# Another common order for 2210 operations of a gated recurrence with an MLP, on one core

## The chip, the cores and the metric

The kernel runs on one core of a Trainium2 chip. A core has five engines that run side by side, each with its own stream of instructions: TensorE (PE) for matrix products, VectorE (DVE) and ScalarE (ACT) for element-wise work, GpSimd (POOL) and SyncE (SP), which here mostly issue DMAs. An engine works through its stream strictly in the order in which the instructions were written down; where an instruction needs something of another engine, it waits for a semaphore, and all that stands behind it on its engine waits too. The metric is the device time of one execution in microseconds (us). A difference of 0.2% is about 1.1 us here.

## The reference

For 4 batches, 8 heads, 768 tokens and 48 channels a head, a gated linear recurrence with complex gates runs over the tokens; its output, laid side by side by heads (384 columns), goes through a low-rank mixing over the tokens (rank 32) and an MLP with a hidden width of 1536.

```python
mag = np.sqrt(a_re * a_re + a_im * a_im)
scale = np.minimum(mag, 0.999) / (mag + 1e-06)
a_re_n, a_im_n = (a_re * scale, a_im * scale)
for t in range(S):
    new_re = ar * S_re - ai * S_im
    new_im = ar * S_im + ai * S_re
    S_re, S_im = (new_re + kv, new_im)
    y[:, :, t] = np.einsum('bhd,bhde->bhe', q[:, :, t], S_re)
# x: y as (batch, token, head*channel)
h = xt @ U @ V
u = x + h.transpose(0, 2, 1)
ch = np.maximum(u @ w_ch1, 0.0) @ w_ch2
return u + ch
```

All of it is in 4-byte floats. `w_ch1` and `w_ch2`, `U` and `V` arrive as 8-byte floats and are turned into 4-byte ones on the chip.

## The kernel before

The 768 tokens of a batch are cut into chunks of 128; there are 24 chunks in all, six to a batch. Two neighbouring chunks make a group (`GROUPS`) for the gates, and two chunks make a token block for the MLP (`mixer`).

The work has these stages. `gates` (line 622) turns the gates of a group into logarithms of magnitudes and angles, sums both over the tokens of a chunk by a product with a triangle of ones (tiles `es ps` and `ph`), and takes exponentials and sines (tiles `es` and `cs`). `prep` (793) weighs the rows of q and k by `es` and `cs` (tiles `qk`, then `QKC`) and transposes them on PE, 16 small transposes at a time (tile `tr`, line 816), which ACT copies to `QK`. `chain` (827) has the products inside a half chunk (`inner`), the state that a chunk adds (`dk`), and the output (`y`), and ACT copies the output to `xo`. `mixer` (918) has the rank products (`rank`, `mixed`), the transposes of the token block (`uTp`), the first MLP layer (`up` for the first two token blocks, `few` for the others: a scheme with fewer products and more additions on DVE), and the second layer (`down`). The 8-byte weights come in by large loads into two staging areas (`single`, 555) and are converted by five instructions a piece, on DVE for the first six pieces and on DVE and ACT for the others. `judge` (1361) counts, from values collected by DVE all along (line 657), whether the inputs left the range for which the fast method holds: PE sums the counts (`count`), and DVE casts the sum to an integer in the tile `flag`. After all operations each engine loads `flag` into a register (line 1395) and branches on it (line 1405); the general method behind the branch does not run for these inputs.

None of these functions emits anything at once. Each call of `PE`, `ACT`, `DVE`, `POOL` or `SP` only registers an operation with the class `Plan`, with the names of what it reads and writes; from the names `Plan.add` works out which earlier operations it needs. Operations are numbered as they are registered, 0 to 2209. At the end the loop over `plan.order()` emits them in the sequence of the tuple `ORDER`, so this tuple fixes the stream of every engine: its operations in the sequence in which they stand in `ORDER`. `order()` also asserts that no operation stands before one that it needs, and that a buffer is not taken before its last user is listed. The waits between engines are not made from the names in the plan: they come from the tiles that the emitted instructions touch, so they are there whatever the plan says. The dictionary `SPARE` has PE emit 34 products without use ahead of operations 125, 135, 199, 209, 223 and 243 (`idle`, 1379), in both kernels.

The operations named below, by number: 91 to 94 load the gates of chunks 0 and 1, 0 loads the triangle, 5 and 11 the first two pieces of `w_ch1`, 18 and 17 `U` and `V`, 28 the third piece, 149 to 152 the gates of group 1, 194 and 195 q and k of chunk 0, 218 and 219 q and k of chunk 1, 196 v of chunk 0. 96 (ACT) and 97, 98 (DVE, lines 654 and 655) start the gates of chunk 0; 99 and 100 (DVE, line 657) collect its range check; 101 to 103 (ACT) and 104, 105 (DVE) end in the logarithm that 109 (PE, `es ps`) sums. 106 to 108 make the angles. 112 to 124 are the same for chunk 1, where 115 and 116 are the range check. 10 and 16 are the last conversions of the first two pieces of `w_ch1`. 198, 202, 222 and 226 (DVE, line 441) make `QKC` for q and k of chunks 0 and 1; 199, 203, 223 and 227 (PE) transpose them. 208 and 209 (`dk`) and 206 (`inner`) are the products of chunk 0. 368 makes `QKC` for k of chunk 4, 369 transposes it. 937, 1475 and 1968 are the rank products of batches 1 to 3. 2208 is the count on PE, 2209 the cast to `flag` on DVE.

Of the kernel before, what the change touches and what calls it, by code (L numbers as in the profile page):

```python
# [316 lines left out]
def kernel(  # L317
# [19 lines left out]
    DM = H * D  # L337
# [53 lines left out]
    def get(*base):  # L391
        if base not in T:
            T[base] = makers[base]()
        return T[base]
# [432 lines left out]
    def chain(i):  # L827
# [84 lines left out]
        for r in range(2):  # L912
            ACT(c_act(HH * D) + 0.04, RR, lambda r=r: nc.scalar.copy(out=halves(get(*xi))[r * HC:(r + 1) * HC, :, 1],
                                                                     in_=get(*y[1])[side(r, 1)]), [y[1] + (r,)], [xi + (r + 1,)])
# [540 lines left out]
```

## Time and profile before

| | us |
|---|---|
| device time, median of 3 runs | 554.59 |
| the runs | 554.28, 554.59, 554.6 |
| span of the profiled execution, first to last instruction | 552.8 |
| of it PE busy | 526.9 (95%) |
| PEld (weight loads, beside PE) busy | 477.3 (86%) |
| DVE busy | 432.8 (78%) |
| ACT busy | 317.8 (57%) |
| POOL busy | 32.2 (6%) |

For the profiled execution the profile gives the span alone, 552.8 us; the median of the runs, 554.59 us, lies 1.8 us above it, since a device time takes in what lies before the first and after the last instruction. The granted TensorE clock was 0.998 of full speed over the span.

In rows of the timeline the first number is the start in us from the beginning of the span, the second the length of the piece in us; then come the engine, the line of the kernel, the operation, the tiles (written <- read), the shape and the count, and in brackets the idle time of the engine before it and what ended it. Instructions of one engine overlap a little, so that the next one starts before the one before it has ended. Matrix products of 4-byte floats show as two records each.

### The profile page before, as it was taken

What the parts mean: (1) busy time and instruction counts of PE and PEld (TensorE: products, weight loads), DVE (VectorE), ACT (ScalarE), POOL (GpSimd) and SP (SyncE); (2) the same over time, 40 slices, a digit from 0 to 9 for tenths busy, and PEclk for the clock granted to TensorE, in tenths of its full rate; (3) what the DMA queues carried; (4) which work ended last, traced back from release to release, by engine and by line L of the source; (5) the groups of instructions that cost most, each with busy time, mean ns of one, the idle gap of its engine ahead of it and who ended that gap; (6) DMA issues with size and microseconds to landing.
All of it is one profiled execution on the core that took longest, in us unless ns stands there. A gap on an engine that the chain in (4) does not pass through costs nothing.

```text
span 552.8 us, 16672 instructions
## 1 busy us (share of the span) xinstructions
PE 526.9 (95%) x7228; PEld 477.3 (86%) x7228; DVE 432.8 (78%) x828; ACT 317.8 (57%) x553; POOL 32.2 (6%) x61
## 2 busy tenths in 40 slices
PE   2899999999999999999999999999999999999996
PEld 1677776767999987999999998999999989999995
DVE  6899989999999987998787987786953635567352
ACT  6889999795597787567827956626512232110100
POOL 1000000001010000102001001002000000000000
PEclk9999999999999999999999999999999999999999
DMA  9988876523441354314513425003300000000001
GB/s 229 187 184 174 195 170 151 144 30 87 88 89 30 56 104 77 59 31 85 91 38 67 74 38 111 2 1 59 59 9 23 17 11 15 8 8 23 21 9 34
DMA packets 150688, 39.92 MB, mean 72 GB/s; under 512 B 145912, under 2 KB 147408, under 8 KB 150608
## 3 DMA queue, kind: packets, MB, share of 16 engines
q1 hardware_dynamic: 148400, 34.43, 31.2%
q0 software_dynamic: 2208, 4.35, 2.3%
q8 instruction: 59, 0.97, 0.7%
q14 instruction: 21, 0.17, 0.1%
HBM read 33.60 MB, written 4.76 MB: 69 GB/s over the span
## 4 chain that ended last, share of the span: by engine, by line
PE 73%; DVE 12%; ACT 4%; issue 2%; DMA 1%; POOL 0%; DVEq 0%; SPq 0%; ACTq 0%; POOLq 0%
PE down L1235 26%; PE few L1103 25%; PE tr L816 4%; PE dk L865 3%; PE inner L845 3%; PE y L902 3%; PE up L991 2%; PE y L894 2%; DVE xo L444 1%; ACT gate L438 1%; PE rank L937 1%; PE ph L755 1%; PE mixed L960 1%; PE uTp L976 1%; PE es ps L691 1%
## 5 line engine op out<-in xcount | busy, mean ns | idle before, releaser
L1111 ACT COPY h<-few 128x512 f32<-128x512 f32 x60 | 35.1, 585 | 87.3 <-PE few L1103 87.1
L1235 PE MATMUL down<-w,h 128*128 128x192 f32 x396 | 72.7, 330 | 0.9 <-DVE xo L444 0.7
L438 ACT ACTIVATE gate<-gate 128x768 f32<-128x768 f32 (+2 forms) x74 | 65.6, 900 | 9.2 <-DVE GS L750 3.8
L1235 PEld LDWEIGHTS down<-w,h 128*128 128x128 f32 x396 | 64.5, 190 | 3.7 <-issue 1.5
L822 ACT COPY QK<-tr 112x512 f32<-112x512 f32 x96 | 49.9, 596 | 17.8 <-PE tr L816 17.7
L444 DVE TENSOR_TENSOR xo<-down,xo 128x192 f32<-128x192 f32 (+1 forms) x79 | 29.9, 385 | 33.9 <-PE down L1235 33.4
L1115 DVE CUSTOM_DVE_ANT_1 h<-few,h 128x512 f32<-128x512 f32 x60 | 40.5, 686 | 15.7 <-PE few L1103 11.8
L1103 PE MATMUL few<-extra,w 128*128 128x128 f32 x400 | 50.9, 276 | 0.0
L1103 PEld LDWEIGHTS few<-extra,w 128*128 128x128 f32 x400 | 48.0, 192 | 0.1
L441 DVE TENSOR_TENSOR QKC<-qk,cs 128x768 f32<-128x768 f32 x48 | 44.4, 950 | 1.7 <-PE dk L865 1.3
L1235 PE MATMUL down<-stage 128*128 128x192 f32 x198 | 37.9, 330 | 0.4 <-DVE xo L444 0.4
L438 ACT ACTIVATE es<-es ps 128x384 f32<-128x384 f32 x48 | 20.1, 502 | 31.2 <-PE es ps L691 29.2
L444 DVE TENSOR_TENSOR h<-few,h 128x512 f32<-128x512 f32 x30 | 20.6, 688 | 20.4 <-ACT h L1111 12.1
L1179 POOL DMA_DIRECT2D out_dram<-xo x32 | 17.9, 558 | 313.8 <-DVE xo L444 297.7
L991 PE MATMUL up<-uT,w 128*128 128x256 f32 x144 | 34.5, 387 | 0.7 <-ACT uT L980 0.7
L1235 PEld LDWEIGHTS down<-stage 128*128 128x128 f32 x198 | 32.3, 190 | 1.7 <-DVE xo L444 1.0
L1103 PE MATMUL few<-gate,w 128*128 128x128 f32 x240 | 32.2, 278 | 0.4 <-DVE gate L1075 0.4
L435 ACT ACT_TABLE_LOAD x24 | 30.8, 1283 | 1.1 <-PEq L1439 0.7
L816 PEld LDWEIGHTS tr<-ident,QKC 64*112 64x112 f32 x768 | 24.2, 130 | 8.3 <-issue 3.6
L816 PE MATMUL tr<-ident,QKC 64*112 64x64 f32 x768 | 28.9, 221 | 2.4 <-DVE QKC L441 2.4
L991 PEld LDWEIGHTS up<-uT,w 128*128 128x128 f32 x144 | 26.4, 190 | 5.3 <-ACT uT L980 0.9
L1103 PEld LDWEIGHTS few<-gate,w 128*128 128x128 f32 x240 | 29.3, 192 | 0.8 <-PE uTp L976 0.6
(161 smaller groups left out, 1100.4 us busy)
## 6 DMA issues: line engine op xcount, KB each, us to landing
stage<-in_moe_w_ch_dram SPq DMA_DIRECT2D x12, 768.0 KB
gate<-in_a_im_dram SPq DMA_DIRECT2D x24, 192.0 KB
gate<-in_a_re_dram SPq DMA_DIRECT2D x24, 192.0 KB
VP<-in_v_dram SPq DMA_DIRECT2D x24, 192.0 KB
qk<-in_q_dram SPq DMA_DIRECT2D x24, 192.0 KB
qk<-in_k_dram SPq DMA_DIRECT2D x24, 192.0 KB
out_dram<-xo POOLq DMA_DIRECT2D x12, 192.0 KB, 2.2
out_dram<-xo POOLq DMA_DIRECT2D x20, 96.0 KB, 2.1
```

Of the source, the lines that this page charges most:

```text
L435: ACT(1.4, rank, lambda: nc.scalar.preload_act_table_set(name), writes=[TABLE])
L438: return nc.scalar.activation(out=o, in_=i, func=f, **kw)
L441: nc.vector.tensor_tensor(out=o, in0=a, in1=b, op=OP.mult)
L444: nc.vector.tensor_tensor(out=o, in0=a, in1=b, op=OP.add)
L816: nc.tensor.transpose(out=get(*ps[r])[0:DQ, h], in_=get(*qkc)[at, h].rearrange("p u d -> p (u d)")[:, 0:DQ], identity=ident[at, at], tile_ ...
L822: nc.scalar.copy(out=get(*QK)[:, u].rearrange("p (h t) -> p h t", t=CH)[:, :, r * HC:(r + 1) * HC], in_=get(*ps[r])[0:DQ])
L991: nc.tensor.matmul(out=get(*ps)[:, e], lhsT=w1[:, f, (ff + e) * 128:(ff + e + 1) * 128], rhs=get(*uT)[:, f], start=(f == 0), stop=(f == KD ...
L1103: nc.tensor.matmul(out=get(*ps)[:, q], lhsT=w()[:, q * 128:(q + 1) * 128], rhs=v[0](), start=(n == 0 and q == 0), stop=True, skip_group_ch ...
L1111: ACT(c_act(n3 * CH) - 0.045, RU, lambda i=i, k=k: nc.scalar.copy(out=at(i, k), in_=get(*ps)), [ps], [o])
L1115: DVE(c_dve(n3 * CH), RU, lambda i=i, k=k: nc.vector._custom_dve(dve_ops.TENSOR_ADD_SAT, out=at(i, k), in0=get(*ps), in1=at(i, k), s0=math ...
L1179: queue.dma_start(out=out[b, c * CH:(c + 1) * CH, lo:hi], in_=get("xo", i)[:, lo:hi])
L1235: nc.tensor.matmul(out=get(*to)[:, part], lhsT=x(j), rhs=y[:, j], start=(first and j == 0), stop=(j == KH - 1), skip_group_check=not first)
```

## The change

The tuple `ORDER` is replaced by another permutation of the same 2210 numbers. Four registrations of operations get further names. The product that reads the piece of `w2` which one DVE instruction rewrites in place now reads a name, `("w2i", 0)`, that this instruction writes; the addition of a `down` product to `xo` reads the name of the PSUM bank as a whole; and the two copies from `y` read both halves of it. No operation is added or removed, none has another body, and each stays on its engine. The new tuple has one line more, so that line numbers below it rise by one.

```diff
 ORDER = (
-    95, 93, 91, 0, 92, 94, 196, 150, 5, 96, 99, 11, 3, 100, 4, 151, 97, 152, 101, 98, 149, 112, 115, 194, 116, 106, 218, 113, 102, 195, 107, 114, 117,
-    104, 219, 108, 103, 315, 118, 105, 122, 1, 120, 109, 119, 220, 123, 121, 267, 111, 124, 125, 110, 316, 7, 6, 317, 126, 127, 8, 2, 133, 9, 128,
-    318, 13, 134, 10, 129, 138, 135, 12, 18, 139, 136, 14, 17, 137, 154, 15, 140, 157, 144, 141, 16, 143, 142, 28, 145, 197, 146, 147, 155, 148, 198,
-    153, 202, 199, 159, 156, 209, 266, 200, 203, 265, 221, 201, 208, 160, 158, 210, 222, 161, 205, 211, 223, 204, 162, 130, 226, 164, 206, 131, 225,
...
-    1849, 1553, 1587, 1554, 1850, 1851, 1573, 1588, 1648, 1852, 1923, 1915, 1593, 1914, 1574, 1583, 1647, 1916, 1576, 1579, 1584, 1853, 2208, 1580,
-    1589, 2209, 1854, 1585, 1582, 1590, 1645, 1595, 1586, 1594, 1591, 1855, 1640, 1873, 1592, 1856, 1869, 1857, 1874, 1597, 1596, 1875, 1870, 1897,
...
-    2188, 2182, 2178, 2185, 2183, 2189, 2199, 2184, 2192, 2190, 2186, 2193, 2187, 2191, 2195, 2194, 2200, 2196, 2201, 2197, 2198, 2202, 2203,
+    91, 93, 99, 95, 96, 97, 98, 94, 92, 100, 101, 0, 102, 104, 115, 112, 113, 114, 5, 152, 106, 103, 117, 105, 116, 3, 4, 118, 120, 119, 122, 107,
+    109, 123, 121, 125, 11, 111, 110, 6, 150, 8, 7, 149, 151, 126, 127, 194, 108, 9, 124, 12, 14, 13, 10, 133, 134, 135, 138, 15, 136, 137, 139, 140,
+    195, 218, 128, 18, 154, 16, 143, 155, 141, 219, 142, 144, 145, 146, 147, 197, 198, 148, 153, 202, 199, 200, 156, 221, 203, 159, 17, 129, 19, 157,
+    205, 222, 196, 160, 201, 204, 226, 162, 20, 161, 223, 28, 315, 209, 220, 227, 225, 224, 164, 1, 131, 228, 163, 208, 2, 165, 210, 130, 167, 318,
...
+    1474, 1473, 1748, 1155, 1162, 1749, 1750, 1789, 1738, 1472, 1156, 1158, 1780, 1160, 1475, 1476, 1164, 1751, 1477, 1481, 1768, 1769, 1770, 1163,
+    1478, 1555, 1165, 1479, 1791, 1556, 1795, 1169, 1559, 1482, 1483, 1480, 1485, 1166, 1170, 1486, 1171, 1492, 1796, 1772, 1797, 1487, 1490, 1560,
...
+    2125, 2182, 2178, 2183, 2199, 2185, 2184, 2188, 2047, 2120, 2192, 2175, 2189, 2186, 2187, 2190, 2193, 2195, 2191, 2194, 2200, 2196, 2197, 2201,
+    2198, 2202, 2203, 2208, 2209,
 )
@@
-                                                                     in_=get(*y[1])[side(r, 1)]), [y[1] + (r,)], [xi + (r + 1,)])
+                                                                     in_=get(*y[1])[side(r, 1)]), [y[1]], [xi + (r + 1,)])
@@
-                    PE(0.975, RM, lambda half=half: products(half), reads(half) + [("w2s", 0)],
+                    PE(0.975, RM, lambda half=half: products(half), reads(half) + [("w2s", 0), ("w2i", 0)],
@@
-                DVE(c_dve(DH if y is not None else DM), R0, f, [ps + (part,)] + ([] if also is None else [ps + (also,)]),
+                DVE(c_dve(DH if y is not None else DM), R0, f, [ps + (part,), ("bank", ps[1])] + ([] if also is None else [ps + (also,)]),
@@
-                                                                    op=OP.subtract), [("w2s", 0)], ALL_W2)
+                                                                    op=OP.subtract), [("w2s", 0)], ALL_W2 + [("w2i", 0)])
```

154 rows, old and new, of the table ORDER are left out of this document.

## The prediction

> **What bounds the kernel now.** First the page: its busy shares and two rows of the 40 slices (busy tenths).
>
> ```profile
> span 552.8 us, 16672 instructions
> PE 526.9 (95%) x7228; PEld 477.3 (86%) x7228; DVE 432.8 (78%) x828; ACT 317.8 (57%) x553; POOL 32.2 (6%) x61
> PE   2899999999999999999999999999999999999996
> DVE  6899989999999987998787987786953635567352
> ```
>
> PE is busy from the second slice to the last, so a reordering can win only what PE does not work: 25.9 us. Where these lie is shown by the view by windows (stretch, its length, then busy time and count of PE, PEld, DVE, ACT, POOL):
>
> ```profile
> 0.00:11.04 11.04, 0.00 (x1) 0.03 (x1) 7.11 (x25) 6.67 (x12) 2.17 (x14) 1.00 0.94 210
> 11.04:25.45 14.41, 11.81 (x62) 9.07 (x62) 12.30 (x21) 11.56 (x20) 0.00 (x0) 1.00 1.10 203
> 25.45:45.03 19.58, 17.88 (x403) 13.66 (x403) 19.58 (x34) 17.25 (x33) 0.00 (x0) 1.00 0.94 189
> 45.03:74.00 28.97, 27.61 (x498) 22.15 (x501) 28.97 (x46) 26.81 (x47) 0.00 (x0) 1.00 0.76 182
> 74.00:200.00 126.00, 124.96 (x1810) 104.75 (x1802) 119.14 (x211) 100.94 (x167) 8.37 (x12) 1.00 0.44 94
> 200.00:290.00 90.00, 87.85 (x1200) 81.78 (x1199) 78.80 (x156) 59.34 (x103) 6.62 (x10) 1.00 0.33 64
> 290.00:403.00 113.00, 112.25 (x1744) 106.11 (x1743) 92.23 (x185) 71.00 (x129) 8.50 (x13) 1.00 0.27 50
> 403.00:548.00 145.00, 144.57 (x1538) 139.74 (x1536) 74.32 (x157) 24.20 (x49) 6.51 (x12) 1.00 0.05 15
> 548.00:552.80 4.80, 0.00 (x0) 0.00 (x0) 0.36 (x1) 0.00 (x0) 0.00 (x0) 0.82 0.22 72
> ```
>
> Length less PE busy gives the idle time: 11.04 before the first product; 2.60, 1.70 and 1.36 up to 74 us (5.66 together); 1.04, 2.15, 0.75 and 0.43 from there to 548 (4.37); 4.80 at the end. DVE is busy for all of 25.45 to 74.00: there the end of a DVE instruction is the sum of what stands ahead of it on DVE, so the order alone sets it. So I go through the start, the stretch up to 74 us, the middle and the end. All terms are made on this execution's span of 552.8; the runs' median is 554.59, and I carry the 1.8 between them unchanged.
>
> **The names of dependencies** emit nothing; waits are made from tiles. Cost: zero. PE's 34 spare products stay ahead of the same operations.
>
> **The start.** The first product needs operation 105 on DVE. From the timeline:
>
> ```profile
> 4.97 0.84 ACT L438 ACTIVATE gate<-gate 128x768 f32<-128x768 f32 x1 [2.95 <-DMA gate<-in_a_re_dram]
> 5.04 0.56 DVE L657 CUSTOM_DVE_ANT_0 low<-gate 128x384 f32<-128x384 f32 x1 [2.40 <-DMA gate<-in_a_re_dram]
> 7.94 0.56 DVE L657 CUSTOM_DVE_ANT_0 low<-gate 128x384 f32<-128x384 f32 x1
> 9.76 0.55 DVE L441 TENSOR_TENSOR gate<-gate 128x384 f32<-128x384 f32 x1
> 10.33 0.56 DVE L444 TENSOR_TENSOR GL<-GL,gate 128x384 f32<-128x384 f32 x1
> 11.04 1.62 PE L695 MATMUL es ps<-GL,prefix_r 128*128 128x384 f32 x2 [11.04 <-DVE GL L444]
> ```
>
> The last DVE row is 105; the two above it are 116 and 108, which the new order puts behind it. That takes away 0.57 each: DVE alone would allow 9.2 instead of 10.33. ACT now does 102 (0.60) ahead of 112, on which 113 and 114, still ahead of 105, wait; this gives back about 0.3. So 105 starts at 9.5 and the first product at 10.2: 0.8 earlier, bounds 0 and 1.1. On SP the same four gate loads come first.
>
> **Up to 74 us.** PE waits here for the products `QKC`, at the three PE rows of line 816 here:
>
> ```profile
> 25.45 0.66 PE L816 MATMUL tr<-ident,QKC 64*112 64x64 f32 x16 [1.65 <-DVE QKC L441]
> 26.43 0.68 PE L865 MATMUL dk<-VP,QKC 64*64 64x48 f32 x32
> 28.80 0.95 DVE L441 TENSOR_TENSOR QKC<-qk,cs 128x768 f32<-128x768 f32 x1
> 29.80 0.66 PE L816 MATMUL tr<-ident,QKC 64*112 64x64 f32 x16 [0.19 <-DVE QKC L441]
> 69.67 0.56 DVE L441 TENSOR_TENSOR G<-G,T 112x384 f32<-112x384 f32 x1
> 70.13 0.96 DVE L655 SCALAR_TENSOR_TENSOR gate<-gate 128x768 f32<-128x768 f32 x1
> 71.00 1.83 DVE L441 TENSOR_TENSOR QKC<-qk,cs 128x768 f32<-128x768 f32 x2
> 72.98 0.66 PE L816 MATMUL tr<-ident,QKC 64*112 64x64 f32 x16 [0.53 <-DVE QKC L441]
> ```
>
> Starts on DVE follow each other by 0.46 for an instruction of 0.56 and by 0.87 for one of 0.96; I count with these steps.
>
> PE operation 199 (first row, 25.45): the same PE work stands ahead in both orders, 11.8 us, so PE gets there at 10.2 + 11.8 = 22.0. DVE has one range check (157, 0.9) less ahead of 198 and starts on its way 0.8 earlier: 23.7 instead of 25.4. PE waits 1.7. Operation 223 (29.80) comes next but one: of the 4.16 us of PE work between them before, the two `dk` (0.6 each) and one spare product (0.46) now stand behind it, so PE is there at 26.2. DVE's 222 ended at 29.75; ahead of it stand 35 operations in both orders, but 158 (0.88) has gone behind it and 19 (0.27) ahead: 28.35. PE waits 2.15, and has now idled 3.85.
>
> Operation 369 (72.98) is the check on the whole stretch: 60 PE operations stand ahead of it in both orders, 56.3 us (72.98 - 11.04 - 5.66) with the spare products. Ahead of 368, which it waits for, the new order has seven DVE operations fewer (388, 596, 597, 598: 0.87 each; 307, 308: 0.47; 177: 0.1) and one more (353, 0.47): 4.0 us less. DVE would be done at 72.83 - 4.0 = 68.8, PE there at 10.2 + 56.3 + 3.85 = 70.35. So PE is the later one: the idle time up to here falls from 5.66 to 3.85. With the start that makes 2.6 us; bounds: 4.1 (PE there when DVE is) and 0 (the DVE work moved away is missing elsewhere). What goes behind is range checks, gate work for later groups and chunk 5's weighing; the longer slack of DVE after 74 us (it idles 6.9 of 126) takes it up.
>
> SP's queue: the moved loads are the same ones. New is that `U` (18) stands ahead of k of chunk 1 (219), and waits for the staging area that 10 frees; the third piece (28) stands ahead of v of chunk 1 and the masks and waits for 16. I cost this at nothing, because 221, the first to need k of chunk 1, starts only at about 25, and the conversions end well before (10 by 17.5); a rival below is what happens without that cover. POOL's moved DMAs likewise, since POOL is 6% busy.
>
> **From 74 to 548 us.** The 4.37 us are small waits with places; three rows of the groups by form:
>
> ```profile
> L960 PE MATMUL mixed<-r,V 64*128 64x192 f32 x96 | 10.8, 343 | 0.3 <-ACT r L943 0.3
> L976 PE MATMUL uTp<-ident,xo 128*128 128x128 f32 x72 | 11.4, 277 | 0.4 <-DVE xo L444 0.3
> L1103 PE MATMUL few<-gate,w 128*128 128x128 f32 x240 | 32.2, 278 | 0.4 <-DVE gate L1075 0.4
> ```
>
> They sit where a batch goes from rank products to the MLP. The new order puts a `down` product between 1475 and its `mixed`, and others between `mixed`, `uTp` and `few`. I take 0.8 of the 1.1 as gone and leave the other waits as they are; bounds: all 4.37 gone, or 1.7 more.
>
> A second cost is the change of PE from one shape of tile to another. From the chain that ended last:
>
> ```profile
> 252.88 0.98 PE down L1235 x6
> 253.86 0.89 PE few L1103 x8
> 266.08 1.04 PE tr L816 x32
> 267.12 1.09 PE few L1103 x8
> 448.14 1.17 PE down L1235 x6
> ```
>
> `few` takes 0.89 after `down`, which has its shape, and 1.09 after `tr`; `down` 0.98 or 1.17. So a change costs 0.2. Counted from the orders there are 165 changes before and 163 after: 0, within 0.4.
>
> **The end.** The count 2208 and the cast 2209 stood in the middle (388 us) and now stand last. Rows of the lines of the load of `flag`, of the branch and of the cast, and the last DVE instruction:
>
> ```profile
> L1395 PEldq TENSOR_LOAD <-flag x1: 487/487/487, 544.9 to 544.9; - x1
> L1405 PEldq COMPARE_BRANCH  x2: 90/1774/3457, 545.5 to 548.2; - x2
> L1377 DVE CAST flag<-bad ps 1x1 int32<-1x1 f32 x1 | 0.1, 136 | 0.0
> 548.02 0.36 DVE L444 TENSOR_TENSOR xo<-down,xo 128x192 f32<-128x192 f32 x1 [0.42 <-PE down L1235]
> ```
>
> PE's sequencer loaded `flag` at 544.9, ahead of its last products, and the long branch ran from 548.2 for 3.46 us to 551.6, 1.2 us before the end. Now with PE's products done at 548.0: the cast follows the last addition (548.4) and ends at 548.55, PE's load takes 0.49 (549.1), the first branch 0.1 and a semaphore as much again, so the long branch starts near 549.45 and ends at 552.9 instead of 551.6: +1.3. Bounds: 0, if what the branch waits for ends at 551.6 anyway, and 1.5. No row says what it does for 3.46 us. [...]
>
> **Sum.** -0.8 (start) - 1.8 (waits up to 74) - 0.8 (batch turns) + 0 (shapes) + 1.3 (end) = -2.1: span 550.7, time 552.5.
>
> **Rivals.**
> *The end hides it.* The long branch is not late, because it waits for something that does not move: 551.2. For it: other branches take 0.1. Against: only PE's is long.
> *The middle clears up.* The waits after 74 fall to 1.5 instead of 3.6: 550.4. For it: DVE has less work ahead of the same products. Against: the places named explain a quarter of them.
> *The middle draws new waits.* 1.7 more than forecast at other places: 554.2, no change. For it: each of 11 token blocks has turns like those that cost 0.3 to 0.4.
> *The loads come late, and it is slower.*
>
> ```profile
> SPq L569 <- DVE w L588: 21.5, 8, 6.1
> ```
>
> SP waited for staging areas 8 times, up to 6.1 us. If 18 holds k of chunk 1 back, then from 2 us of delay (219 is issued at about 18.5; the earliest loads, issued from 0.73, were used at 5.0, so it is there near 22.9, and 221 wants it at 25) each us stands in PE's way; the forecast's gain is used up at 4.1. With the longest wait of 6.1: 552.5 + 4.0 = 556.5. For it: the DMA share is 0.94 and more up to 45 us. Against: before, no `QKC` waited for a load there.
> That the new names do nothing is certain, and part of the forecast.
>
> **How the numbers follow.** A difference under 0.2%, 1.1 us, cannot be told from none: faster is below 553.5, slower above 555.7. Forecast 0.42 (its own range 551.2 to 553.5), end hides it 0.15, middle clears 0.09, new waits 0.14, late loads 0.20. Faster 0.66, same 0.14, slower 0.20. The range goes from 549.6 (the two good cases together, in part) to 556.6 (late loads with the longest wait); what it leaves out is several bad turns together.
>
> **What would show it.** The first product at 10.2; two waits of PE for `QKC` before 29 us and none near 70; operation 369 near 70.4; PE idle 74 to the last product near 3.6 us; PE's load of `flag` behind its last product, and 6.1 instead of 4.8 us from there to the end. A wait of DVE on `qk` for a DMA near 25 us, or PE idle above 6 us between 11 and 74, would make it wrong.

## The result, and the profile after

The new order is slower: 557.91 us (median of 10 runs, 555.65 to 562.19) against 555.06 for the kernel before (10 runs, 554.2 to 556.71), a ratio of 1.0051 with a 95% interval of 1.003 to 1.0071. The prediction was 552.5, in a range up to 556.6: the sign was wrong, and the time lies outside.

The page of the changed kernel, the same rows as before the change:

```profile
span 556.0 us, 16656 instructions
PE 524.2 (94%) x7228; PEld 475.3 (85%) x7228; DVE 432.2 (78%) x828; ACT 317.8 (57%) x553; POOL 31.9 (6%) x61
PE   2799999999999999999999999999999999999992
DVE  6999989999989898898897967687676644657350
```

PE, DVE, ACT and POOL run as many instructions as before (7228, 828, 553 and 61), PE is even busy for 2.7 us less, and yet the span grew by 3.2. The last digit of the PE row tells where to look: 2 tenths instead of 6 in the last slice of 14 us. The view by windows of the changed kernel, cut at its first product, at the old marks and at its last product (stretch, length, then busy time and count of PE, PEld, DVE, ACT, POOL, then granted clock, DMA share, GB/s):

```profile
0.00:10.31 10.31, 0.00 (x1) 0.04 (x1) 5.99 (x22) 5.81 (x10) 2.15 (x14) 1.00 0.90 216
10.31:74.00 63.69, 58.59 (x1018) 46.49 (x1018) 62.71 (x101) 58.47 (x105) 0.00 (x0) 1.00 0.85 177
74.00:200.00 126.00, 121.98 (x1757) 101.84 (x1759) 116.80 (x204) 99.67 (x163) 7.72 (x11) 1.00 0.46 99
200.00:290.00 90.00, 88.57 (x1332) 82.59 (x1327) 80.35 (x158) 62.48 (x109) 6.51 (x10) 1.00 0.29 56
290.00:403.00 113.00, 112.58 (x1504) 107.47 (x1503) 83.90 (x169) 60.71 (x107) 8.22 (x13) 1.00 0.28 54
403.00:545.70 142.70, 142.51 (x1635) 136.88 (x1633) 82.20 (x179) 30.61 (x63) 7.33 (x13) 1.00 0.07 17
545.70:556.00 10.30, 0.00 (x0) 0.00 (x0) 0.25 (x2) 0.00 (x0) 0.00 (x0) 0.69 0.11 36
```

Length less PE busy, beside the forecast of each term:

| | idle or busy before | after | change | forecast |
|---|---|---|---|---|
| to the first product | 11.04 | 10.31 | -0.73 | -0.8 |
| from there to 74 us | 5.66 | 5.10 | -0.56 | -1.8 |
| 74 us to the last product | 4.37 | 6.06 | +1.69 | -0.8 |
| PE busy | 526.92 | 524.25 | -2.67 | 0 |
| last product to the end | 4.80 | 10.30 | +5.50 | +1.3 |
| span | 552.8 | 556.0 | +3.2 | -2.1 |

So the products themselves are done 2.3 us earlier than before (545.7 against 548.0, the two products of the count among them), and the 5.5 us behind them eat that and more. What stands there is told by the rows of POOL's own sequencer. Lines of the load of `flag`, of the branch and of the kernel's end, first in the changed kernel, then in the one before (durations in ns as least, median and most, then first and last start in us):

```profile
L1396 POOLq TENSOR_LOAD <-flag x1: 601/601/601, 546.0 to 546.0; - x1
L1406 POOLq COMPARE_BRANCH  x2: 38/39/40, 546.7 to 548.3; - x2
L1406 POOLq INC_SWDGE_SEM  x1: 1123/1123/1123, 547.2 to 547.2; - x1
L1451 POOLq DRAIN  x3: 46/112/3973, 551.1 to 555.7; - x3
L1406 PEldq COMPARE_BRANCH  x2: 90/1985/3880, 546.7 to 547.0; - x2
```

```profile
L1395 POOLq TENSOR_LOAD <-flag x1: 492/492/492, 535.5 to 535.5; - x1
L1405 POOLq COMPARE_BRANCH  x2: 38/39/40, 536.1 to 538.8; - x2
L1405 POOLq INC_SWDGE_SEM  x1: 1123/1123/1123, 537.6 to 537.6; - x1
L1450 POOLq DRAIN  x3: 46/112/3974, 541.3 to 552.5; - x3
```

After `flag` is read, POOL goes through 0.6 us of loading, some semaphores, 1.1 us of INC_SWDGE_SEM, a branch, 2.8 us without a record and a DRAIN of 4.0 us: 9.1 us from 546.0 to 555.1, and 0.9 us of common ending follow. In the kernel before POOL had nothing left to do from 535.5, found `flag` long written, and went through the same steps beside PE's last products: it was done at 545.2, before they were. The cast as the last operation of all puts the whole of it behind the last product. PE's long branch, on which the forecast rested, ran from 547.0 to 550.9, and nobody waited for it.

### The profile page after: what moved, and what is told of

Read it like the earlier page. It is cut to its first block, busy times and chain, and to the rows that moved or that the text cites. A ratio compares the mean times of both kernels' runs of the same rounds, so it can differ in the third digit from the quotient of the medians.

```text
span 556.0 us, 16656 instructions
## 1 busy us (share of the span) xinstructions
PE 524.2 (94%) x7228; PEld 475.3 (85%) x7228; DVE 432.2 (78%) x828; ACT 317.8 (57%) x553; POOL 31.9 (6%) x61
## 4 chain that ended last, share of the span: by engine, by line
PE 66%; DVE 13%; issue 7%; ACT 6%; DMA 5%; SPq 1%; POOL 0%; DVEq 0%; ACTq 0%; POOLq 0%
PE down L1236 23%; PE few L1104 21%; DMA gate<-F 3%; PE y L903 3%; PE dk L866 3%; PE down L1193 3%; PE inner L846 3%; PE tr L817 2%; ACT gate L439 2%; PE y L895 2%; DMA gate<-in_a_im_dram 2%; DVE QKC L442 1%; PE rank L938 1%; PE mixed L961 1%; PE uTp L977 1%
## 5 line engine op out<-in xcount | busy, mean ns | idle before, releaser
L823 ACT COPY QK<-tr 112x512 f32<-112x512 f32 x96 | 52.0, 593 | 29.2 <-PE tr L817 29.0
L1180 POOL DMA_DIRECT2D out_dram<-xo x32 | 19.9, 666 | 214.3 <-DVE xo L445 145.4
L817 PE MATMUL tr<-ident,QKC 64*112 64x64 f32 x768 | 27.9, 220 | 3.5 <-DVE QKC L442 3.5
```

Source lines behind the costliest of these rows:

```text
L817: nc.tensor.transpose(out=get(*ps[r])[0:DQ, h], in_=get(*qkc)[at, h].rearrange("p u d -> p (u d)")[:, 0:DQ], identity=ident[at, at], tile_ ...
L823: nc.scalar.copy(out=get(*QK)[:, u].rearrange("p (h t) -> p h t", t=CH)[:, :, r * HC:(r + 1) * HC], in_=get(*ps[r])[0:DQ])
L1180: queue.dma_start(out=out[b, c * CH:(c + 1) * CH, lo:hi], in_=get("xo", i)[:, lo:hi])
```

## Experiments on the end

**The count early, in the new order.** Nothing else is moved.

```diff
 ORDER = (
...
-    2133, 1706, 2042, 2043, 2135, 2138, 2097, 2108, 2110,
+    2133, 1706, 2042, 2043, 2135, 2138, 2097, 2208, 2209, 2108, 2110,
...
-    2202, 2203, 2208, 2209,
+    2202, 2203,
```

> The new order, with the count 2208 and the cast 2209 put ahead of PE operation 2108, 35 us before the last product; nothing else. Theory 'the ending of GpSimd' (POOL): after it has the flag, POOL needs 9.1 us to the end of its long DRAIN (545.99 to 555.11 in the new kernel; 535.51 to 545.25, beside PE's work, in the kernel before), so a late flag puts all of that behind the last product. With an early flag POOL ends near 545, the 4.8 us of the kernel before follow the last product at 545.5, and the span is 550.3 instead of 556.0: 5.7 less than the new kernel, a time near 552.3. Theory 'PE's branch' (that of the prediction): only PE's load of the flag and long branch move, 1.3 less, 556.6. If the tail is not the cause, no change, 557.9.

552.29 us, a ratio to the kernel before of 0.9932 (0.9908 to 0.9956): 3.7 us less than it, measured beside it, and 5.6 less than the median of the new kernel (6.6 by the two ratios to the kernel before). "The ending of GpSimd" said 552.3, "PE's branch" 556.6.

```profile
L1396 POOLq TENSOR_LOAD <-flag x1: 503/503/503, 537.9 to 537.9; - x1
L1451 POOLq DRAIN  x3: 46/112/3973, 544.2 to 553.6; - x3
```

POOL's long DRAIN starts at 544.2 and is through at 548.2, beside PE's products again (the last one ended at 548.9 in this execution, 3.3 us later than in the new kernel's: 0.6 of it stands already at 24 us, some 1.3 come with a fall of the clock that is told below, and 0.7 with a longer wait at 85 us). Behind the last product there are 4.97 us instead of 10.30.

**The count last, in the old order.** The mirror image.

```diff
-    1849, 1553, 1587, 1554, 1850, 1851, 1573, 1588, 1648, 1852, 1923, 1915, 1593, 1914, 1574, 1583, 1647, 1916, 1576, 1579, 1584, 1853, 2208, 1580,
-    1589, 2209, 1854, 1585,
+    1849, 1553, 1587, 1554, 1850, 1851, 1573, 1588, 1648, 1852, 1923, 1915, 1593, 1914, 1574, 1583, 1647, 1916, 1576, 1579, 1584, 1853, 1580,
+    1589, 1854, 1585,
...
-    2202, 2203,
+    2202, 2203, 2208, 2209,
```

> The old order, with 2208 and 2209 put last; nothing else. 'The ending of GpSimd': 0.2 for the two products, and 10.3 instead of 4.8 us from the last product to the end: 5.7 more than the kernel before, near 560.8. 'PE's branch': 1.3 more, 556.4. Tail not the cause: 555.1.

561.12 us, a ratio of 1.0088 (1.0068 to 1.0107), 5.2 us more than the kernel before on the same chip; behind the last product there are 10.34 us instead of 4.82. The old order pays the same price.

**The flag 4 us before the end.** The pair stands ahead of 2195 in the new order, otherwise as in the first experiment.

```diff
-    2190, 2193, 2195, 2191,
+    2190, 2193, 2208, 2209, 2195, 2191,
...
-    2202, 2203, 2208, 2209,
+    2202, 2203,
```

> The new order, with 2208 and 2209 ahead of PE operation 2195, so that the flag is there near 541.8 instead of 545.95, still before the last product at 545.5. 'The ending of GpSimd': POOL's DRAIN ends 9.1 us after that, at 550.9, the last 0.9 us follow: a span of 551.8, 4.2 less than the new kernel (about 553.7 as a time), between the new kernel and the one with the early count. 'PE's branch': what PE does is finished with the flag there before the last product, so the same as with the early count. A rival by which any place but the last frees the whole of it says the same as with the early count too.

553.14 us, a ratio of 0.9951 (0.993 to 0.9972). As a time it is within the noise of the early count, so the medians alone don't separate the theories by 1.4 us. The trace does, by a little: POOL read the flag at 542.1, its DRAIN ran from 546.9 to 550.8, the span ended at 551.7, where 551.8 was expected. PE's DRAIN had been through 0.8 us earlier, DVE's only 0.25:

```profile
L1396 POOLq TENSOR_LOAD <-flag x1: 496/496/496, 542.1 to 542.1; - x1
L1451 POOLq DRAIN  x3: 46/112/3974, 546.9 to 551.4; - x3
L1451 PEldq DRAIN  x2: 8/38/68, 549.9 to 551.2; - x2
L1451 DVEq DRAIN  x2: 10/34/58, 550.5 to 551.1; - x2
```

From the last product to the end the span has 5.6 us here, between the 4.8 to 5.3 us of twelve traces with an earlier flag (all but that of the next experiment) and the 10.3 of the two with the flag last.

**POOL alone late.** The early count, and the last of the output transfers goes to POOL's queue. The flag is early for every engine; only POOL has something to wait for.

```diff
             if m == B * NCH // MC - 1:
-                SP(0.6, ("load", 0), lambda: f(nc.sync), [o], [("out", i)])
+                (POOL if y == 1 else SP)(0.6, ("load", 0), lambda: f(nc.gpsimd if y == 1 else nc.sync), [o], [("out", i)])
```

> As the one with the early count, but the last of the output transfers (192 columns of the last chunk) is issued by POOL instead of SyncE. The flag is early for all engines; POOL alone is held back, until the last addition to xo at 545.9. 'The ending of GpSimd': its issue takes 0.5, the wait for its landing about 2, then 1.1 (INC_SWDGE_SEM), 2.7 without a record, 4.0 (DRAIN) and 0.9: an end near 557, 6 to 7 us later than with the early count, with PE's branch where it is there. [...]

560.46 us, a ratio of 1.0084 (1.006 to 1.0109): 8.2 us more than with the early count, where 6 to 7 were expected; the transfer landed 2.8 us after its issue, not 2. PE's long branch started at 546.3, near the place it has with an early flag, and POOL's ending came last:

```profile
L1396 POOLq TENSOR_LOAD <-flag x1: 491/491/491, 547.0 to 547.0; - x1
L1451 POOLq DRAIN  x3: 46/112/4055, 553.8 to 558.4; - x3
L1406 PEldq COMPARE_BRANCH  x2: 90/1905/3720, 543.6 to 546.3; - x2
```

That settles the end: it is POOL's own ending, 9 to 11 us from its load of the flag, and not PE's branch.

## Experiments on PE's wait at 26 us and the clock

The runs of the new order spread over several us. The traces show one cause. PE waits 1.78 us ahead of 223; the profiled execution with the early count had that wait as well (1.80), and 1.7 us after its end the granted clock fell to half for 3.41 us, which the new kernel's own profile does not show. Two experiments change the length of that wait and nothing else, by the number of spare products ahead of 223, both with the early count.

```diff
 SPARE = {
-    125: 2, 135: 10, 199: 14, 209: 1, 223: 5, 243: 2,
+    125: 2, 135: 10, 199: 14, 209: 1, 223: 11, 243: 2,
 }
```

> The kernel with the early count, with 11 instead of 5 spare products ahead of PE operation 223, where PE waits 1.78 us: 5 of them took 1.38, so 6 more take 1.66 and fill the wait. Theory 'clock': in the kernels with the early count and with the count 4 us before the end the granted clock fell to 0.5 for 3.41 us from 30.2 and 28.9, behind that wait, which costs 1.7 us there; in the new kernel and in the one whose last transfer is POOL's it did not fall. With the wait filled it never falls: the fastest execution as with the early count (550.1), the median about 1 lower and the spread smaller. Rival: the fall has nothing to do with the wait: the clock still falls in some executions, and the median stays at 552.3.

```diff
 SPARE = {
-    125: 2, 135: 10, 199: 14, 209: 1, 223: 5, 243: 2,
+    125: 2, 135: 10, 199: 14, 209: 1, 243: 2,
 }
```

> The new order with the early count and no spare product ahead of 223 (5 in the new kernel), so that PE waits there 3.2 us. 'Clock': the granted clock falls to 0.5 for one or two stretches of 3.41 us in the profile, and in nearly all executions: a median of 553.5 to 555, 1.3 to 3 above that with 5 products, 2.5 to 4 above that with 11. Rival, spare products only cost time: 552.3 or less.

With 11 products 551.01 us (0.9919, 0.9902 to 0.9935), with none 554.71 (0.9984, 0.997 to 0.9997), with 5 it had been 552.29. The step from none to 11 is clear of the noise; that from 5 to 11 is in the medians and the spread (550.18 to 552.16 against 550.09 to 555.71), but the two intervals overlap. The mean granted clock of all executions agrees: 0.991 to 0.994 without spare products, 0.994 to 1.000 with 5, 0.998 to 1.000 with 11. The row of PE's wait and the clock in two stretches behind it, without spare products and then with 11 (in the windows the granted clock stands third from the end):

```profile
28.25 0.53 PE L817 MATMUL tr<-ident,QKC 64*112 64x64 f32 x5 [3.18 <-DVE QKC L442]
26.30:29.70 3.40, 1.45 (x18) 1.35 (x18) 3.40 (x8) 2.88 (x6) 0.00 (x0) 0.50 0.46 44
29.70:33.10 3.40, 3.40 (x83) 2.91 (x82) 2.97 (x7) 2.49 (x5) 0.00 (x0) 0.50 0.76 151
```

```profile
24.61 2.72 PE L1388 MATMUL tr<-ident 128*128 128x128 f32 x22
27.77 0.66 PE L817 MATMUL tr<-ident,QKC 64*112 64x64 f32 x16 [0.44 <-DVE QKC L442]
26.30:29.70 3.40, 2.96 (x72) 2.55 (x72) 3.40 (x7) 3.40 (x7) 0.00 (x0) 1.00 0.37 31
29.70:33.10 3.40, 3.40 (x84) 2.47 (x82) 3.40 (x8) 3.40 (x8) 0.00 (x0) 1.00 0.96 175
```

PE does work without use from 24.61 to 27.3 instead of waiting, transposes at the same time (27.77 against 28.25), and keeps the full clock. At 37 us the kernel without spare products is 2.2 us behind the one with 11 (0.4 of it from the start), at the last product 3.4.

All sixteen traces of this case together, by PE's wait and the clock in or behind it:

| PE's wait | number of such waits | clock fell to 0.50 |
|---|---|---|
| up to 1.5 us | all other waits behind the first product | never |
| 1.65 to 1.80 us, at 24 to 28 us | 9, in nine executions | in 5: for 3.41 us in 4, for 6.83 in 1 |
| 2.1 to 6.8 us | 6, in five executions | in 6: for 3.41 us in 2, for 6.83 in 4 |

The nine are those of the kernel before, of the one with the count last and of the new rest behind the old head (1.65), and of the new kernel, the early count, the count 4 us early, POOL late, and the first and the third of the joined orders below (1.78 to 1.80). The kernel before and the new one are among those whose clock did not fall in the profiled execution, so the fall is no part of the 3.2 us between the two traces; it is part of their spread. The falls lasted 3.41 us or twice that, 6.83. Behind the waits of 1.65 us the clock fell in one execution of three, behind those of 1.78 to 1.80 us in four of six; in the new kernel and with POOL late it stayed full behind 1.78. So the length of the wait is not all that counts; what else does is not known.

**The old order with its wait filled.** The same for the kernel before, whose wait of 1.65 us stands ahead of 199.

```diff
-    125: 2, 135: 10, 199: 14, 209: 1, 223: 5, 243: 2,
+    125: 2, 135: 10, 199: 20, 209: 1, 223: 5, 243: 2,
```

> The old order with 20 instead of 14 spare products ahead of PE operation 199, where PE waits 1.65 us; nothing else. 'Clock': in the executions of the kernel before above 555 the clock falls behind that wait, as it did with the old head and the new rest (0.5 for 3.41 us from 27.6). With the wait filled the median goes to that of its undisturbed executions, 554.3, and the spread narrows. Rival, the spread has another cause: 555.6 as before.

556.71 us, a ratio of 1.0021 (1.0 to 1.0042): a miss. The clock stayed full in the profile and the median still did not come down, nor did the spread (554.69 to 561.26). So the spread of the kernel before has another cause as well. The executions of the kernel before that ran beside it say the same: nine of the 34 had a mean granted clock below 0.997, and their median is 1.0 us above that of the others (556.35 against 555.32), but the others alone still go from 554.46 to 557.86. In the trace with the wait filled PE lost 1.2 us at `mixed`, and a transfer stands at the head of that chain, in the timeline:

```profile
337.34 0.82 POOL L741 DMA_DIRECT2D gate<-F  x1 [0.79 <-DVE F L764]
342.27 0.36 DVE L749 CAST GS<-gate 128x384 fp32r<-128x384 f32 x1 [1.76 <-DMA gate<-F]
345.16 1.08 PE L960 MATMUL mixed<-r,V 64*128 64x192 f32 x9 [1.50 <-ACT r L943]
```

The cast of L749 starts 4.9 us after POOL issued `gate<-F`. In the kernel before, whose instructions are the same there, it was 3.8 us (337.21 and 341.04), and PE waited 0.28 for `r`. That landing, 1.1 us later, can account for the 1.2 us. It is one pair of traces; what makes the landing differ stays open.

## Experiments on the head and the middle

**Parts of the two orders joined.** At 90 PE operations both orders have done the same ones (94.4 us in the new kernel, 97.4 in the one before), and again at 194 (193.4 and 193.0). In the traces PE of the new kernel is 3.0 us ahead at the first of these marks, 0.4 behind at the second, and 2.3 ahead at the end. Three kernels join the orders there: a part of one, then what is left in the sequence of the other.

The lines at the cuts: the first against the new order, the second against the old one, the third against the first.

```diff
-    430, 690, 453, 65, 499, 624, 450, 416, 625, 626, 66, 627,
+    430, 690, 453, 65, 499, 624, 343, 713, 637, 790, 66, 643, 67, 644, 616, 68, 69, 72, 618, 422, 625, 619, 639, 500,
...
-    415, 449, 624, 453, 499, 69, 72, 618, 422, 625, 619, 639,
+    415, 449, 624, 453, 499, 690, 450, 416, 625, 626, 627, 417, 500,
...
-    894, 1225, 868, 876, 898, 1226, 896, 918, 877, 581, 1219,
+    894, 1225, 868, 876, 898, 896, 1226, 918, 877, 922, 878, 879, 900, 1219,
```

> The new order for its first 442 entries (the first 90 operations of PE, the same 90 in both orders; PE is through them at 94.4 us in the new kernel, at 97.4 in the one before), and from there the old order, the count in the middle with it. If the head keeps its gain: 3.0 us less than the kernel before. If the gain is borrowed, because 2.4 us of DVE's work (67, 68, 343, 643, 644, less 690) is put off past the cut and PE then waits for it: 0.6 less. If the loss of the new kernel in the middle comes from the head: no gain.

> The old order for its first 451 entries (the same 90 operations of PE), from there the new one, with the count 35 us before the end. In the new kernel PE is 3.0 us ahead at that point and 2.5 ahead at its last product: the new rest costs 0.5 more than the old one. If the two parts are independent: 0.5 more than the kernel before. If the waits of the new rest come from what the new head has put off: 1 to 2 us less than the kernel before.

> The new order to the first cut (94 us), the old one from there to the first 194 operations of PE (193 us), the new one from there, with the early count. In the new kernel PE is 3.0 us ahead at the first cut, 0.4 behind at the second and 2.5 ahead at its last product: the parts that gain put together give 3.0 + 2.9 = 5.9 less than the kernel before, near 550. If the gain of the head is only borrowed: 3.5 less.

New head and old rest: 563.34 us, 1.0141 (1.0122 to 1.016). Three parts: 561.05, 1.0113 (1.0082 to 1.0144). Both are far slower than either order, which none of the theories had said. The timeline of DVE and PE in the first of them shows why:

```profile
97.08 0.17 DVE L711 TENSOR_TENSOR least<-least,T 112x16 f32<-112x16 f32 x1
100.73 0.96 DVE L657 CUSTOM_DVE_ANT_0 low<-gate 128x768 f32<-128x768 f32 x1 [3.49 <-DMA gate<-in_a_im_dram]
...
105.43 0.69 PE L755 MATMUL ph<-GS,prefix_r 128*128 128x384 f32 x1 [6.75 <-DVE GS L750]
```

The range check 643 was put off by the new head; the joined order has it directly behind the cut, where its gates have only just been asked for. DVE waits 3.49 us for them, 625, which PE needs, queues behind, and PE waits 6.75 us; from 103.0, still inside this wait, the clock is halved for 6.83 us. In both traces the clock had also fallen behind the wait at 26 us, for 6.83 and 3.41 us. So these two times are the price of my seam and of the clock, and say nothing on the head.

Old head and new rest, with the early count: 554.25 us, 0.9982 (0.9971 to 0.9993), 1.4 less than the kernel before on the same chip, as the second theory had it (1 to 2 less), and not 0.5 more. In its trace the clock fell behind the old wait, so that PE was 1.7 us behind the kernel before at the first mark; from there to the second mark it lost 1.6, and from the second to the last product it gained 3.9. So from 193 us on the new order is better than the old one in both traces that have it (by 2.7 and 3.9). Between the marks it is worse by itself, and of the 3.4 that the new kernel loses there, some 1.8 come only with its own head. One execution stands for each of these numbers, and PE comes to the first mark 4.7 us later here than in the new kernel, which leaves DVE more time; so this split of the 3.4 is not shown.

**Joined without the seam.** The first and the third again, with the eight operations that the new head puts off standing as far behind the cut as in the new order, and with the wait at 26 us filled.

The line at the first cut against that of the first try, and the spare products:

```diff
-    499, 624, 343, 713, 637, 790, 66, 643, 67, 644, 616, 68, 69, 72, 618, 422, 625, 619, 639, 500,
+    499, 624, 67, 66, 68, 69, 72, 616, 618, 422, 625, 637, 619, 639, 500,
...
-    125: 2, 135: 10, 199: 14, 209: 1, 223: 5, 243: 2,
+    125: 2, 135: 10, 199: 14, 209: 1, 223: 11, 243: 2,
```

> The new head and the old rest again, cut at the same place, with two differences: eight of the operations that the new order puts off past the cut (66, 343, 616, 637, 643, 644, 713, 790) stand as far behind the cut as in the new order, not right at it, and 11 spare products stand ahead of PE operation 223. If the 6.75 us wait of the first try was made by the cut (643 and what stands behind it on DVE ahead of 625), it is gone, and the head keeps its gain: 3.0 under an undisturbed run of the kernel before (554.2), 551.2 to 552. If the gain of the head is borrowed: 553.5 and more. If the head itself is what costs the new kernel its time after 94 us: 554 and more.

> New head, old middle (94 to 193 us), new rest with the early count, joined in the same way, with 11 spare products ahead of 223. If the parts add: 2.9 less than new head and old rest, 548.3 to 549. If the waits between 94 and 193 us in the new kernel are the price of its head, the old middle has them too: 551, as the whole new order with the wait filled.

557.95 us (1.0051, 1.0026 to 1.0076) and 555.66 (0.9996, 0.9978 to 1.0014): a miss again. Both have the head's lead at 87 us (PE is 2.6 and 3.6 us ahead of the kernel before), and both are 1.6 behind at 103 us, after a wait of 2.39 for the product `ph` that ends at 98 us and a clock halved in it or behind it (for 3.41 and 6.83 us). So the head's gain could not be carried over to the old middle in any of four tries. It fits a head that borrows from DVE, but each try had a new place of the put-off operations, so this is not shown.

**Six operations moved ahead in their own queues.** This keeps the whole new order, with the early count and 11 spare products, and only takes six operations, for which PE waits after 73 us, ahead of work on their own engine for which PE does not wait. The rows that led to it, from the kernel with 11 spare products:

```profile
133.25 0.36 DVE L750 CAST GS<-gate 128x384 fp32r<-128x384 f32 x1 [1.36 <-DMA gate<-F]
134.12 0.55 DVE L445 TENSOR_TENSOR xo<-down,xo 128x384 f32<-128x384 f32 x1
134.73 2.64 PE L992 MATMUL up<-uT,w 128*128 128x256 f32 x11 [0.72 <-DVE xo L445]
```

The addition to `xo` had all it needed at 128.5. It stood behind a cast that waited for a transfer.

```diff
-    716, 696, 676, 460, 677, 445, 727,
+    716, 696, 445, 676, 460, 677, 727,
...
-    759, 758, 680, 478, 510, 479, 699,
+    759, 758, 479, 680, 478, 510, 699,
...
-    528, 777, 531, 536, 529, 804, 778, 534, 821, 822,
+    528, 821, 777, 531, 536, 529, 804, 778, 534, 822,
...
-    1242, 1214, 1215, 953, 1236, 968, 970,
+    1242, 968, 1214, 1215, 953, 1236, 970,
...
-    618, 77, 458, 644, 648, 455, 426,
+    618, 455, 77, 458, 644, 648, 426,
...
-    594, 52, 370, 376, 597, 393, 688, 367, 257, 371, 366, 372,
+    366, 594, 52, 370, 376, 597, 393, 688, 367, 257, 371, 372,
```

> The new order with the early count and 11 spare products ahead of 223; on top of it six operations move ahead on their own engine, past work that PE does not wait for: on DVE 445 past 676 and 677, 479 past 680, 478 and 510, 821 past 777, 804 and 778, 968 past 1214, 1215 and 953; on ACT 455 past 77 and 648, 366 past 594, 370, 367 and 371. Each had been ready before it ran (445: ready 128.5, run at 134.1; 968: 224.4 and 227.5), and 676, 777 and 1214 wait on DVE for a transfer. PE's waits behind them were 0.72, 0.38, 0.36, 1.08, 0.67 and 0.34, 3.55 together. Theory 'the new waits after 74 us are operations that queue behind others on DVE and ACT': 2.5 to 3.5 less than without the moves (551.0), 547.5 to 548.5. Rival, the work that is passed becomes late instead, or the waits are of DVE's total load: under 1 less, 550 to 551.

550.49 us, a ratio of 0.9903 (0.9884 to 0.9923). The last product ends 0.8 us earlier than with the wait filled alone, a third of what was expected at least. The waits behind 445, 479 and 821 are gone, 1.46 together. The other three came back: behind 968 PE now waits for ACT, behind 455 0.60 instead of 0.67, and moving 366 ahead lengthened its wait from 0.34 to 0.65:

```profile
228.51 1.16 PE L1104 MATMUL few<-gate,extra 128*128 128x128 f32 x8 [0.75 <-ACT h L1112]
```

The last experiment, against the one with the six moves:

```diff
-    17, 129, 19, 157, 205, 222, 196, 160, 201, 204, 226, 162,
+    17, 129, 205, 222, 196, 160, 201, 204, 226, 19, 157, 162,
...
-    759, 758, 479, 680, 478, 510, 699,
+    759, 758, 680, 478, 510, 479, 699,
...
-    125: 2, 135: 10, 199: 14, 209: 1, 223: 11, 243: 2,
+    125: 2, 135: 10, 199: 14, 209: 1, 223: 7, 243: 2,
```

> As the last one, and the range check 157 and the conversion step 19 go behind 226 on DVE, so that 222, which ran at 26.8 and was ready at 25.7, makes QKC of chunk 1 about 1.1 earlier; 7 spare products ahead of 223 instead of 11, for the wait is that much shorter. Expected by the same theory: a further 1.0 less, near 547. Rival, 157 behind 226 is late for nothing but the next operation that PE needs: no further gain, or a loss up to 0.9.

551.57 us, 0.9918 (0.9902 to 0.9934): no further gain. 223 was 0.6 us earlier, and from 30.05 us PE waited 0.87 for `GL` of the next group, which now comes late: a wait moved by one place. Two more things differ. Operation 479 stands at its old place again, which the expectation does not say, and with it PE's wait of 0.39 us at 147 us is back; and at 160 us PE waited 1.03 us for a load of v. So this run does not test its own step alone. Of the 3.55 us of waits that the six moves aimed at, 1.46 were of the place of single operations on DVE; two of these three operations (1.08 us) stood behind a cast that waits for `gate<-F`, the third behind other work. The rest moved when it was pushed at.

The best kernel of the study is the one with the six moves: 0.9903 of the kernel before, 550.49 us. Its interval overlaps that of the new order with the early count and 11 spare products (0.9902 to 0.9935), so the gain of the moves is seen in the trace alone.

## Why the prediction was wrong

*The end* is the step that failed, and it turned the sign: +1.3 was forecast, +5.50 measured. The term was made from PE's long branch, "what the branch waits for", with bounds of 0 and 1.5. That the whole 1.3 would count, and not 0, was an estimate; no run shows it as a lengthening of the span, and what the runs show in its place is POOL's ending. The question was right, what else is still to be done once `flag` is known, but it was asked of PE and DVE alone. POOL's ending stood in the trace of before at 535.5 to 545.2, hidden by PE's products; the cast, moved behind the last product, uncovered the whole of it, 9.1 us in the new kernel. The first two experiments measured 5.6 and 5.2 for that one move; in their traces the part behind the last product differs by 5.3 and 5.5. The rival "the end hides it" went the wrong way as well. Without this step the sum would have been -3.4; with the early count the measured gain over the kernel before is 3.7, though not by the same terms. PE's long branch itself did what was forecast: in the new kernel it ended 5.2 us behind the last product instead of 3.7. But POOL ended another 4.2 behind it. The branch took 3.4 to 4.1 us with an early flag and 3.4 and 3.9 with a late one, so it did not wait for something that stays where it is; what fills it is not known.

*The start*: right. 105 started at 9.61 instead of 10.33 (9.5 forecast), the first product at 10.31 (10.2).

*Up to 74 us*: the check was met, but by luck. 369 was forecast at 70.35 and started at 69.96, where the kernel before has 72.98:

```profile
23.24 0.66 PE L817 MATMUL tr<-ident,QKC 64*112 64x64 f32 x16 [0.33 <-DVE QKC L442]
27.86 0.66 PE L817 MATMUL tr<-ident,QKC 64*112 64x64 f32 x16 [1.78 <-DVE QKC L442]
69.96 1.11 PE L817 MATMUL tr<-ident,QKC 64*112 64x64 f32 x32
```

No wait for `QKC` near 70, as said. But the term of -1.8 rests on a wrong reading: it took the whole 5.66 us of idle time for waits for `QKC`. In the kernel before these were 2.37 (the 1.65, 0.19 and 0.53 of the three rows); the other 3.3 were for `ph`, `uT` and the like, two of them here:

```profile
45.03 4.15 PE L991 MATMUL up<-uT,w 128*128 128x256 f32 x18 [0.66 <-ACT uT L980]
63.64 0.91 PE L758 MATMUL ph<-gate,prefix_z 128*128 128x384 f32 x2 [0.83 <-ACT gate L438]
```

In the new kernel the waits for `QKC` are 2.32 (0.33, 0.21 and 1.78, all before 29 us), and 2.78 us of other waits stand beside them, for `ph`, `uT` and `y` among others. So the waits that were forecast to fall stayed, and the idle time fell by 0.56. From the first product to 369 PE idled 4.8 us, where 3.85 was forecast, and worked 54.9, where 56.3 was forecast; the two errors nearly cancel. Of the single waits, that at 199 was 0.33 instead of 1.7: the forecast had PE there at 22.0, but short waits for `ph` ahead of it, 1.18 us in all (0.95 in the kernel before), brought it there at 22.9. At 223 it was 1.78 instead of 2.15, and 0.21 at 203 was not forecast.

*PE's busy time*: forecast unchanged within 0.4, measured 2.67 less, for the same instructions. By the groups it lies with `tr` (28.9 to 27.9), `mixed` (10.8 to 10.3), `dk` (27.7 to 27.2 for its first half), `rank` and `uTp` (0.3 each). 1.4 of it lies ahead of 369. The count of shape changes, 165 and 163, did not tell it, and no experiment separated its causes: this term stays open.

*From 74 us on*: wrong. The places named did clear up: in front of `mixed` and `uTp` PE waits no more, and the wait of `few` on L1075 is gone. But others came, 0.55 to 1.14 us each at 81, 108, 134, 166, 220 and 228 us: +1.69, against -0.8. That is the rival "the middle draws new waits", which allowed for 1.7 more than forecast; it was 2.5. The moves above show what makes those at 134 and 166 us and a smaller one at 147: the place of one addition or one `QKC` on DVE, at 134 and 166 us behind a cast that waits for a transfer. These casts wait longer in the new order. DVE's waits for `gate<-F`, in us in all, number and longest, in the kernel before and in the new one:

```profile
DVE GS L749 <- DMA gate<-F: 3.2, 4, 1.4
DVE GS L750 <- DMA gate<-F: 11.2, 7, 3.2
```

The fifteen transfers take 1.9 us to land in the median in the kernel before and 2.9 in the new one. No experiment changed that alone, so how much of the +1.69 it makes is not known.

*Late loads*: did not happen; no `QKC` waited for a load before 74 us. *The names*: the instruction counts of PE, DVE, ACT and POOL are the same.

## What to carry to other kernels

Before moving a step behind the last product, list for every engine, POOL and its sequencer included, what it still does after that step, and where it did it before: here 9.1 us of POOL that had run beside PE's products came to stand behind them, and the time grew by 5.2 to 5.6 us. A flag that all engines read belongs far enough ahead that the engine with the longest ending (here POOL, 9.1 us, less the 4.8 that PE and SyncE need anyway) is through with the products. And a wait of PE behind which the clock is halved can be worth filling with products without use: it gained 3.7 us for a wait of 3.2; for the wait of 1.8 the gain is not clear of the noise, and for that of 1.65 in the old order there was none.

## What the runs showed of the hardware that was not expected

- POOL's ending, from the start of its load of the flag to the end of its DRAIN, takes 8.7 to 9.2 us where its last transfer lies 7 us and more back, 9.7 to 10.8 where it has only just been issued; INC_SWDGE_SEM (1.12 to 1.14 us) and the DRAIN (3.97 to 4.06) have the same length in both cases. What fills the 2.5 to 3.0 us without a record between them is not known.
- The granted clock fell to 0.50 in or behind waits of PE of 1.65 to 1.80 us in five executions of nine, for 3.41 or 6.83 us; with 2.1 us and more at all six waits, up to 1.5 us at none.
- A transfer that POOL issued at 337 us (`gate<-F`) landed after 3.8 us in one execution and 4.9 in another, of kernels that do not differ there; the fifteen transfers of this kind took 1.8 to 4.0 us in the kernel before, 1.9 to 4.0 in the new one, with medians of 1.9 and 2.9.
